# Batch 0's first 32 rows of a Fourier transform stored from even partitions, weights loaded behind these stores, and later casts of two constants

## The chip, the cores and the metric

The kernel runs on one core of one Trainium2 chip. The metric is device time in microseconds (us), lower is better. Work on the core is spread over TensorE (PE in the profile, its weight loads PEld), VectorE (DVE), ScalarE (ACT), GpSimd (POOL) and SyncE (SP), which here does nothing but issue DMAs. Each engine runs its own instructions in order; a DMA that SP has issued moves on 16 DMA engines while SP goes on to the next.

## What is computed

Eight batches of 3136 x 256 numbers go through a real Fourier transform along the 3136 rows, a complex 256 x 256 linear layer with bias and soft threshold, the inverse transform, and then a sparse feed-forward layer on the 128 rows with the highest score.

```python
X = np.fft.rfft(x, axis=1)
Yr = Xr @ w_r - Xi @ w_i + b_r;  Yi = Xr @ w_i + Xi @ w_r + b_i
Yr = np.sign(Yr) * np.maximum(np.abs(Yr) - lam, 0.0)      # Yi likewise
y = np.fft.irfft(Y, n=x.shape[1], axis=1)
# per batch: the 128 rows with the highest y @ w_gate
xe = y[b, top_idx];  h = np.maximum(xe @ w1, 0.0);  ye = h @ w2
out[b, top_idx] = xe + sigmoid(score)[:, None] * ye
```

## The kernel before, in words

**Stages.** 3136 is split as 49 x 64. For one batch, stage 1 (`s1`, matmuls of line 397) is a 49-point transform in 8 units `i` of [128 partitions x 8 x 128]; partitions 0 to 63 and 64 to 127 hold the two halves of the 256 columns, and in each half 49 rows are real and 15 are padding. Each unit is copied out of PSUM by ACT (line 412, half of it) and DVE (line 413, the other half) and stored to a scratch tensor `As` in DRAM, so that stage 2 can read it back with rows and columns exchanged (`av`, line 145). Stage 2 (`s2`, line 445, PSUM tile `px`) is the 64-point transform of a group `g` of four rows; there are 13 groups a batch, and one `av` pair (one DMA for each half) serves two groups. Its result is split into a rounded part `Xh` (ACT) and a rest `Xl` (DVE, and POOL for its negated copy), `spectral` multiplies it with the weights in three products each (lines 203 to 205, PSUM tile `py`), `shrink_a`, `shrink_b`, `shrink_c` add the bias, apply the threshold and split again into `Yh` and `Yl` (POOL), and `s2i` does the inverse 64-point transform with the table `gip` (PSUM tile `s`, again lines 203 to 205). `s1i` is the inverse 49-point transform. The feed-forward layer (`prepare`, `hidden`, `combine`) runs between these stages and at the end.

**Steps.** The main loop runs 104 steps `t`, one for each group of each batch. In step `t` PE does `s2` of group t + 1, `spectral` of group t and `s2i` of group t - 2, and from time to time units of `s1` for a later batch and of `s1i` for an earlier one. Inside the loop PE, ACT, DVE and SP are held to the order in which the code is written (`ordered`); POOL is not. `av` is loaded 3 steps ahead (`AP`), x units 4 steps (`XP`).

**The beginning.** Ahead of the loop SP issues, in this order: the 8 x units of batch 0, a piece of the stage-2 table `g_sb`, and then, as `s1` of batch 0 delivers its units, stores. Units 0 and 1 are stored whole (512 KB each). Of units 2 to 7 the rows 0 to 15 of each half are stored first, which is two DMAs of 16 partitions (64 KB) a unit, and the rows 16 to 63 later, two of 48 partitions (192 KB). The weights `w_r` (tile `r1`) and `w_i` (tile `Yl`) are loaded between the first stores. Then come x unit 1 of batch 1, the bias, and the first `av` pair, which reads rows 0 to 7 of all units and so has to wait for all of the first stores. `s1` of the units 0 and 1 of batch 1 and the split of the weights stand ahead of stage 2.

**The casts.** The inverse table `gip` is made in 7 pieces: a piece is loaded into a tile `gi` of one buffer, copied with rounding by ACT (line 174), and the rest is taken by POOL (line 175). At an odd step `t` the load, the ACT copy and the POOL instruction of a piece are written one after another. The same holds for the 8 pieces of `w2` (load into `xe`, ACT line 195, POOL line 196), one at every even step from 24 to 38.

Of the kernel before, what the change touches and what calls it, by code (L numbers as in the profile page):

```python
# [10 lines left out]
F32 = mybir.dt.float32  # L11
# [65 lines left out]


def _places():
# [17 lines left out]
def fourier_moe(ctx: ExitStack, tc: tile.TileContext, x, w_r, w_i, bri, wg, w1, w2,  # L97
# [69 lines left out]
    def ld_gi(k):  # L167
        s = slice(4 * k, min(4 * k + 4, NJ))
        t = pool.tile([128, s.stop - s.start, 128], F32, name="gi", bufs=1)
        ld(t, t_gi[:, s])  # L170
        return t, s

# [9 lines left out]
    def consts_moe(k):  # L182
# [6 lines left out]
        elif k == 1:  # L189
            ld(w1s, w1.rearrange("(h p) f -> p h f", p=128))  # L190
        else:
            f = k - 2
            t = pool.tile([128, D], F32, name="xe", bufs=3)
            ld(t, w2[128 * f:128 * f + 128])
            nc.scalar.copy(out=w2h[:, f, :], in_=t)
            nc.gpsimd.tensor_tensor(out=w2l[:, f, :], in0=t, in1=w2h[:, f, :].bitcast(F32), op=ALU.subtract)

# [206 lines left out]
    def s1(b, i):  # L404
        if i == 0:
            As[b] = dram.tile([2, 64, N2, 128], F32, name="As")
        n = ("at", "at", "at", "ct", "ct", "ot", "ot", "ot")[i] if b == 0 else "at"
        a = pool.tile([P, 8, 128], F32, name=n, bufs=2 if n == "ct" else 3)
        p = [ps.tile([P, 4, 128], F32, name="s", bufs=4) for _ in range(2)]
        xi = xt.pop((b, i))  # L410
        tiles4(p, w1f, lambda r, c: xi[64 * r:64 * r + N1, :, 128 * c:128 * c + 128])
        nc.scalar.copy(out=a[:, :4, :], in_=p[0])
        nc.vector.tensor_copy(a[:, 4:, :], p[1])  # L413
        if t >= 0:
            store(As[b].rearrange("h q n d -> (h q) n d")[:, 8 * i:8 * i + 8, :], a)
        else:
            made.append((b, i, a))

    made = []

    def st_a(b, i, a, q=slice(0, 64)):
        to = As[b][:, :, 8 * i:8 * i + 8, :]
        if q == slice(0, 64):
            ld(to.rearrange("h q n d -> (h q) n d"), a)
        else:
            for h in range(2):
                ld(to[h, q], a[64 * h + q.start:64 * h + q.stop])

    def ld_a(b, g):
        if g == G - 1:  # L430
            av[b, g] = pool.tile([64, 2, 1, 128], F32, name="av", bufs=3)
            ld(av[b, g][:, :, 0], As[b][:, N1 - 1].rearrange("h n d -> n h d"))
        elif g % 2 == 0:
            av[b, g] = av[b, g + 1] = pool.tile([128, 2, 4, 128], F32, name="av", bufs=3)
            for h in range(2):
                ld(av[b, g][:, h], As[b][h, 4 * g:4 * g + 8].rearrange("(j q) n d -> (q n) j d", q=2))

# [112 lines left out]
    HB, YB = 2, 3  # L550
    G, U, ORD = 13, 8, 0
    PE, ACT, DVE, SP = [getattr(mybir.EngineType, n) for n in ("PE", "Activation", "DVE", "SP")]
# [104 lines left out]
    loaded = [U + 2]  # L657
    ws = []

# [13 lines left out]
    t = -1  # L673
# [12 lines left out]
    s1(1, 0)  # L686
    s1(1, 1)
    split_w(ws[0], wrh, wrl)
    split_w(ws[1], wih, wil)
    add_bias()  # L690
    ld_a(0, 0)
    ld_a(0, 1)
    gi = ld_gi(0)
# [6 lines left out]
    for u in made[5:8]:  # L700
        st_a(*u, slice(16, 64))
    for u in made[8:]:
        st_a(*u)
    for t in range(-1, B * G):
# [123 lines left out]
```

## Time and profile before

| | |
|---|---|
| median of 3 runs | 713.37 us (712.81 to 713.53) |
| profiled execution, its own time | 713.84 us |
| its span | 712.1 us |
| PE busy | 676.7 us (95 %) |
| DVE, ACT, POOL busy | 468.1, 384.6, 210.0 us |
| mean granted clock of TensorE | 0.983 of 2.4 GHz |

The span is what the profile shows from the first instruction to the last; 1.74 us of the execution's own time lie around it. In the rows further down a `timeline` line gives start, duration, engine, line of the code, operation, output and inputs, and in brackets how long the engine stood idle just before and what ended that. A windows line gives for one stretch the busy time of PE, PEld, DVE, ACT and POOL (in brackets the count of instructions), then the granted clock of TensorE as a share of 2.4 GHz (0.50 is 1.2 GHz), the mean busy share of the 16 DMA engines, and GB/s moved. A chain line gives start, duration and what ran.

### The profile page before, as it was taken

The page shows a single profiled execution, that of the slowest core. Times are in us where ns is not written, and L with a number is a line of the kernel's source. Part 1 is how long each engine was busy: PE and PEld are TensorE (multiplying, and loading weights), DVE is VectorE, ACT ScalarE, POOL GpSimd, SP SyncE. Part 2 cuts the span into 40 slices and gives each one's busy share as a digit, 9 for nine tenths or more (in the row PEclk, how much of TensorE's full clock was granted, in tenths as well). Part 3 has the DMA queues.
Part 4 walks back from the last instruction along what each step waited for, and adds up shares of the span by engine and source line. Part 5 has one row for each costly group of instructions (what it writes and reads, how often), then busy time and mean ns, then how long its engine had stood idle before and what let it go on. Part 6 is the DMA issues. An engine that isn't in the chain of part 4 may idle for free.

```text
span 712.1 us, 15039 instructions
## 1 busy us (share of the span) xinstructions
PE 676.7 (95%) x5482; PEld 556.7 (78%) x5482; DVE 468.1 (66%) x1330; ACT 384.6 (54%) x759; POOL 210.0 (29%) x255
## 2 busy tenths in 40 slices
PE   7499999999999999999999999999999999998997
PEld 2288788998888689878987888887877887886666
DVE  3256666566655555565677877777897789966752
ACT  3145565565564665666666556665556454445541
POOL 1024433324332323322223322222322322232231
PEclk9689999999999899999999999999999999999999
DMA  9989987788789899989999999997877765646960
GB/s 334 303 299 343 357 247 232 245 276 274 243 301 331 287 318 314 328 292 343 327 299 298 333 321 316 305 307 244 260 239 223 221 206 185 196 158 219 379 238 24
DMA packets 146551, 195.29 MB, mean 274 GB/s; under 512 B 8725, under 2 KB 111278, under 8 KB 146478
## 3 DMA queue, kind: packets, MB, share of 16 engines
q1 hardware_dynamic: 145422, 192.10, 81.2%
q0 software_dynamic: 912, 2.21, 1.0%
q8 instruction: 43, 0.70, 0.4%
q14 instruction: 30, 0.25, 0.1%
q10 hardware_dynamic: 144, 0.03, 0.0%
HBM read 100.58 MB, written 93.85 MB: 273 GB/s over the span
## 4 chain that ended last, share of the span: by engine, by line
PE 72%; DVE 11%; DMA 7%; issue 4%; ACT 3%; POOL 1%; SPq 1%; POOLq 0%; DVEq 0%; ACTq 0%
PE s L397 13%; PE py L203 11%; PE py L204 11%; PE px L445 11%; PE py L205 11%; PE s L203 3%; PE s L204 3%; PE s L205 3%; DMA gi<-t_gi 3%; DVE py L472 2%; PE py L351 2%; DMA xe<-in_moe_w 2%; DVE yf L479 1%; DVE Xl L450 1%; PE s L351 1%
## 5 line engine op out<-in xcount | busy, mean ns | idle before, releaser
L487 POOL TENSOR_TENSOR Yl<-yf,Yh 128x512 fp32r<-128x512 f32 (+1 forms) x104 | 130.3, 1253 | 343.2 <-ACT Yh L486 337.0
L474 ACT ACTIVATE r<-py,m2l 128x512 f32<-128x512 f32 (+1 forms) x104 | 69.8, 671 | 157.4 <-DVE py L472 154.4
L472 DVE TENSOR_TENSOR py<-py,bias 128x512 f32<-128x512 f32 (+1 forms) x104 | 70.4, 676 | 106.0 <-PE py L205 100.9
L445 PEld LDWEIGHTS px<-g_sb,av 128*128 128x128 f32 (+1 forms) x800 | 99.7, 194 | 39.1 <-DVE at L413 20.8
L203 PE MATMUL py<-wrh,Xh 128*128 128x256 f32 x400 | 122.9, 307 | 0.0
L445 PE MATMUL px<-g_sb,av 128*128 128x128 f32 (+1 forms) x800 | 115.6, 287 | 5.9 <-DVE Xl L450 4.6
L204 PE MATMUL py<-wrh,Xl 128*128 128x256 f32 x400 | 113.3, 283 | 0.0
L205 PE MATMUL py<-wrl,Xh 128*128 128x256 f32 x400 | 113.2, 283 | 0.0
L203 PE MATMUL py<-wih,Xh 128*128 128x256 f32 x400 | 113.0, 282 | 0.0
L204 PE MATMUL py<-wih,Xl 128*128 128x256 f32 x400 | 112.9, 282 | 0.1
L205 PE MATMUL py<-wil,Xh 128*128 128x256 f32 x400 | 112.3, 281 | 0.0
L450 DVE TENSOR_TENSOR Xl<-px,Xh 128x512 fp32r<-128x512 f32 (+1 forms) x104 | 69.5, 669 | 42.9 <-ACT Xh L449 31.3
L518 DVE CUSTOM_DVE_ANT_0 junk<-ct,wgb 128x256 f32<-128x256 f32 (+1 forms) x200 | 90.6, 453 | 6.2 <-ACT ct L505 3.2
L505 ACT COPY ct<-s 128x512 f32<-128x512 f32 (+1 forms) x104 | 59.4, 572 | 52.3 <-PE s L205 50.4
L397 PE MATMUL s<-xt,w1f 49*64 49x512 f32 x480 | 68.5, 648 | 12.8 <-DMA xt<-in_x 7.8
L203 PEld LDWEIGHTS py<-wrh,Xh 128*128 128x128 f32 x400 | 76.5, 191 | 2.0 <-issue 1.0
L204 PEld LDWEIGHTS py<-wrh,Xl 128*128 128x128 f32 x400 | 76.6, 191 | 0.9 <-issue 0.9
L205 PEld LDWEIGHTS py<-wrl,Xh 128*128 128x128 f32 x400 | 76.4, 191 | 0.0
L204 PEld LDWEIGHTS py<-wih,Xl 128*128 128x128 f32 x400 | 76.0, 190 | 0.3 <-POOL Xl L451 0.3
L203 PEld LDWEIGHTS py<-wih,Xh 128*128 128x128 f32 x400 | 76.0, 190 | 0.0
L205 PEld LDWEIGHTS py<-wil,Xh 128*128 128x128 f32 x400 | 75.9, 190 | 0.0
L479 DVE SCALAR_TENSOR_TENSOR yf<-py,r 128x512 f32<-128x512 f32 (+1 forms) x104 | 69.5, 668 | 8.0 <-ACT r L474 4.2
(125 smaller groups left out, 1197.4 us busy)
## 6 DMA issues: line engine op xcount, KB each, us to landing
xt<-in_x SPq DMA_DIRECT2D x60, 512.0 KB, 6.1
As<-at SPq DMA_DIRECT2D x58, 512.0 KB, 4.1
cv<-As SPq DMA_DIRECT2D x58, 512.0 KB, 5.5
out<-ot SPq DMA_DIRECT2D x57, 512.0 KB, 3.6
av<-As SPq DMA_DIRECT2D x96, 256.0 KB, 5.0
As<-ct SPq DMA_DIRECT2D x96, 256.0 KB, 4.9
out<-at SPq DMA_DIRECT2D x7, 512.0 KB, 6.9
xt<-As SPq DMA_DIRECT2D x6, 512.0 KB, 5.3
```

The source lines that it names most:

```text
L203: nc.tensor.matmul(out, wh, mh, start=start, stop=False)
L204: nc.tensor.matmul(out, wl, mh, start=False, stop=False)
L205: return nc.tensor.matmul(out, wh, ml, start=False, stop=stop).ins
L397: last_mm = nc.tensor.matmul(out[r][64 * c:64 * c + 64], w[64 * r:64 * r + N1, :], src(r, c), start=True, stop=True)
L445: nc.tensor.matmul(px[:, 2 * p + h, :], a[:, h, 2 * (g % 2) * (w - 1) + p, :], g_sb[:r, 2 * g + p, :], start=True, stop=True)
L450: nc.vector.tensor_tensor(out=xl[:, :, NF:], in0=px, in1=xh[:, :, NF:].bitcast(F32), op=ALU.subtract)
L472: nc.vector.tensor_tensor(out=p, in0=p, in1=bias[:, :w, :], op=ALU.add)
L474: nc.scalar.activation(out=r1[b, g], in_=p, func=AF.Relu, bias=m2l, scale=1.0)
L479: nc.vector.scalar_tensor_tensor(out=yf, in0=py.pop((b, g)), scalar=0.0, in1=r1.pop((b, g)), op0=ALU.min, op1=ALU.add)
L487: nc.gpsimd.tensor_tensor(out=yl, in0=yf, in1=yh.bitcast(F32), op=ALU.subtract)
L505: nc.scalar.copy(out=c, in_=p)
L518: nc.vector.tensor_tensor_reduce(out=junk[:r], in0=c[:, k, :], in1=wgb[:r], scale=1.0, scalar=0.0, op0=ALU.mult, op1=ALU.add, accum_out=Cs ...
```

## The change

**Batch 0's stage 1** uses a second copy of its table, `w1p`, with the columns in another order (`_parity`): rows 0 to 31 of each half come out in the even partitions, rows 32 to 48 and the padding in the odd ones. `w1p` is loaded on ACT's queue ahead of `w1f`. The even partitions of a unit (64 partitions, 256 KB) are stored in one DMA to a DRAM tensor `early`, the odd ones later, in one DMA, to `late`. `av` of batch 0 reads from these. `As[0]` is left for the inverse; its padding rows are filled by two DRAM-to-DRAM copies (`pads`, 480 KB each) at steps 14 and 16.

**Order at the beginning.** All eight `early` stores come before the two weight loads, and the first `av` pair comes right behind the weights, ahead of x unit 1 of batch 1, the bias and the next piece of `g_sb`. `s1` of unit (1, 1) and the bias instructions move into step 0, behind `s2` of group 1.

**Casts.** A `gi` piece is loaded into one of the four buffers of `cv`; pieces 0 and 1 ahead of the loop, the others at steps 1, 3, 5, 7, 9. The ACT copy and POOL instruction of the next piece in line are written at the end of step 0 and of each odd step from 1 to 11, so from piece 2 on two steps behind the load. `w2` pieces are loaded as before and split at the end of steps 28, 30, ... 42, four steps behind the load. `gi` and `w2` casts are now in ACT's fixed order.

```diff
@@ s1, st_a, pads, ld_a
-        n = ("at", "at", "at", "ct", "ct", "ot", "ot", "ot")[i] if b == 0 else "at"
-        a = pool.tile([P, 8, 128], F32, name=n, bufs=2 if n == "ct" else 3)
+        n = ("at", "at", "at", "ct", "ct", "ot", "ot", "ot")[i] if b == 0 else "cv" if b == 1 and i < 2 else "at"
+        a = pool.tile([P, 8, 128], F32, name=n, bufs={"ct": 2, "cv": 4}.get(n, 3))
...
-        tiles4(p, w1f, lambda r, c: xi[64 * r:64 * r + N1, :, 128 * c:128 * c + 128])
+        tiles4(p, w1f if b else w1p, lambda r, c: xi[64 * r:64 * r + N1, :, 128 * c:128 * c + 128])
...
+    def st_a(i, k):
+        ld((early, late)[k].rearrange("h q n d -> (h q) n d")[:, 8 * i:8 * i + 8, :], made[i][k::2])
+
+    def pads(h):
+        ld(As[0][h, N1:].rearrange("p (i n) d -> i p (n d)", n=8), x[0, :, 64 * h + N1:64 * h + 64].rearrange("i p m d -> i p (m d)"))
...
+        src = As[b] if b else early if g < 8 else late
+        q = 4 * g - (0 if b or g < 8 else 32)
@@ ahead of the loop
         s1(0, i)
-        st_a(*made[-1], slice(0, 64 if i < 2 else 16))
-        if i < 2:
-            ws.append(ld_w(*((w_r, "r1", 1), (w_i, "Yl", YB))[i]))
-        if i == 0:
+        st_a(i, 0)
+        if i == 1:
             ld_x(1, 0)
+    ws = [ld_w(w_r, "r1", 1), ld_w(w_i, "Yl", YB)]
+    s1(1, 0)
+    split_w(ws[0], wrh, wrl)
+    split_w(ws[1], wih, wil)
+    ld_a(0, 0)
+    ld_a(0, 1)
     ld_x(1, 1)
     ld(bias, bri)
...
+    ld_gi(0)
+    for i in (3, 0, 1, 2, 4):
+        st_a(i, 1)
     ld(wgb, wg)
...
@@ the loop
-        if t % 2 and (t + 1) // 2 in range(1, 6):
-            consts_gi(*ld_gi((t + 1) // 2 + 1))
+        if t % 2 and (t + 3) // 2 in range(2, 7):
+            ld_gi((t + 3) // 2)
...
+        if t in (14, 16):
+            pads((t - 14) // 2)
...
-        if t < 0:
-            consts_gi(*gi)
-            consts_gi(*ld_gi(1))
+        if t == 0:
+            ordered(s1, 1, 1)
+            add_bias()
...
+        if t == 0 or t % 2 and (t + 1) // 2 in range(1, 7):
+            ordered(consts_gi, *gis.pop(0))
+        if t in range(28, 28 + 2 * (FF // 128), 2):
+            ordered(split_w2, (t - 28) // 2)
```

SP's order at the beginning, from the table piece to the first `av` pair, before (`r` and `Yl` are the weights, `As<-at`, `As<-ct` and `As<-ot` the stores):

```order
L145 DMA g_sb<-t_g 128x512
L145 DMA As<-at 128x1024
L145 DMA r_117<-in_w_r 128x2x256
L145 DMA xt<-in_x 128x1024
L145 DMA As<-at 128x1024
L145 DMA Yl<-in_w_i 128x2x256
L145 DMA As<-at 16x1024 x2
L145 DMA As<-ct 16x1024 x4
L145 DMA As<-ot 16x1024 x6
L145 DMA xt<-in_x 128x1024
L145 DMA bias<-in_b 128x512
L145 DMA av<-As 128x4x128 x2
```

And the same stretch now:

```order
L157 DMA g_sb<-t_g 128x512
L157 DMA early<-at 64x1024 x2
L157 DMA xt<-in_x 128x1024
L157 DMA early<-at 64x1024
L157 DMA early<-ct 64x1024 x2
L157 DMA early<-ot 64x1024 x3
L157 DMA r_193<-in_w_r 128x2x256
L157 DMA Yl<-in_w_i 128x2x256
L157 DMA av<-early 128x4x128 x2
L157 DMA xt<-in_x 128x1024
L157 DMA bias<-in_b 128x512
```

Fourteen stores became eight, the weights moved behind all of them, and x unit (1, 1) and the bias moved behind the `av` pair.

PE's order from batch 0's stage 1 to the first spectral product, before and then now (`s<-xt` and `s<-cv` are units of stage 1, four matmuls a unit; `px` is stage 2):

```order
L397 MATMUL s<-xt,w1f 64x512 x16
L397 MATMUL s<-cv,w1f 64x512 x16
L397 MATMUL s<-xt,w1f 64x512 x8
L445 MATMUL px<-g_sb,av 128x128 x8
L203 MATMUL py<-wrh,Xh 128x256
```

```order
L415 MATMUL s<-xt,w1p 64x512 x16
L415 MATMUL s<-cv,w1p 64x512 x16
L415 MATMUL s<-xt,w1f 64x512 x4
L463 MATMUL px<-g_sb,av 128x128 x8
L415 MATMUL s<-xt,w1f 64x512 x4
L221 MATMUL py<-wrh,Xh 128x256
```

Unit (1, 1) moved from ahead of the first two stage-2 groups to behind them; from there on PE's order is the same.

ACT's order around one `w2` cast of batch 2's part of the program (`at`: copy of a stage-1 unit, `ot`: copies of an inverse unit, `Xh`: split of `px`), before and then now:

```order
L474 ACTIVATE r_2762<-py,m2l 128x512
L412 COPY at<-s 128x512
L195 CAST w2h<-xe 128x256
L547 COPY ot<-s 128x4x128 x2
L448 CAST Xh<-px 128x4x128
```

```order
L492 ACTIVATE r_2754<-py,m2l 128x512
L430 COPY at<-s 128x512
L565 COPY ot<-s 128x4x128 x2
L466 CAST Xh<-px 128x4x128
L467 ACTIVATE Xh<-px 128x4x64
```

The cast that stood between the copies `at` and `ot` is gone from this place; the casts now stand at the ends of later steps.

## Rows read from the trace of the kernel before

**Rows 1.** The page, 40 slices of the span: clock granted to TensorE, in tenths.

```profile
PEclk9689999999999899999999999999999999999999
```

**Rows 2.** Windows by stage: PE, PEld, DVE, ACT, POOL busy; clock; DMA share; GB/s.

```profile
0.00:20.00 20.00, 14.04 (x72) 4.83 (x72) 6.93 (x17) 6.02 (x10) 1.82 (x10) 1.00 0.93 343
20.00:33.40 13.40, 4.36 (x16) 2.19 (x16) 3.47 (x6) 2.40 (x5) 1.26 (x1) 0.59 0.91 280
33.40:39.53 6.13, 6.12 (x28) 6.12 (x29) 0.69 (x1) 0.87 (x2) 0.81 (x2) 0.50 1.01 352
39.53:100.00 60.47, 56.94 (x470) 48.29 (x469) 37.76 (x77) 34.49 (x68) 24.09 (x26) 1.00 0.92 309
100.00:230.50 130.50, 130.22 (x1101) 115.58 (x1101) 80.11 (x195) 75.44 (x148) 45.21 (x56) 1.00 0.85 275
230.50:241.00 10.50, 9.81 (x43) 5.85 (x41) 3.88 (x9) 6.43 (x14) 3.90 (x5) 0.67 0.70 237
241.00:450.00 209.00, 208.63 (x1771) 174.57 (x1773) 141.39 (x358) 128.38 (x254) 60.83 (x75) 1.00 0.96 318
```

**Rows 3.** Timeline of SP's issues: stores and the first `av` pair.

```profile
10.42 0.33 SPq L145 DMA_DIRECT2D As<-at  x1
19.98 2.71 SPq L145 DMA_DIRECT2D As<-ot  x6
22.78 0.37 SPq L145 DMA_DIRECT2D xt<-in_x  x1
23.83 0.93 SPq L145 DMA_DIRECT2D av<-As  x2
```

**Rows 4.** Timeline of ACT and PE around the first stage-2 groups.

```profile
17.94 0.58 ACT L412 COPY ot<-s 128x512 f32<-128x512 f32 x1 [0.32 <-PE s L397]
29.97 1.65 PE L445 MATMUL px<-g_sb,av 128*128 128x128 f32 x6 [0.45 <-DMA av<-As]
33.41 2.08 PE L445 MATMUL px<-g_sb,av 128*128 128x128 f32 x8 [1.78 <-DVE Xl L450]
```

**Rows 5.** Windows at the beginning, same columns: the DMA queue around the first stores.

```profile
15.00:20.00 5.00, 3.98 (x30) 1.19 (x22) 3.20 (x6) 2.24 (x5) 0.00 (x0) 1.00 1.05 411
21.00:22.00 1.00, 0.00 (x0) 0.00 (x0) 0.69 (x1) 0.00 (x0) 0.00 (x0) 1.00 0.71 127
24.00:25.00 1.00, 0.00 (x0) 0.00 (x0) 0.00 (x0) 0.00 (x0) 0.00 (x0) 0.50 0.93 209
25.00:30.00 5.00, 2.73 (x11) 0.86 (x11) 1.12 (x2) 0.00 (x0) 0.00 (x0) 0.50 0.96 309
```

**Rows 6.** Timeline of ACT and PE where casts of `gip` wait for `gi`.

```profile
50.65 0.46 PE L445 MATMUL px<-g_sb,av 128*128 128x128 f32 x2 [0.46 <-DMA av<-As]
55.09 0.62 ACT L174 CAST gip<-gi 128x512 fp32r<-128x512 f32 x1 [2.20 <-DMA gi<-t_gi]
56.82 1.16 PE L445 MATMUL px<-g_sb,av 128*128 128x128 f32 x8 [1.05 <-DVE Xl L450]
87.06 1.16 PE L445 MATMUL px<-g_sb,av 128*128 128x128 f32 x8 [1.35 <-DVE Xl L450]
```

**Rows 7.** Timeline of PE and ACT around a `w2` cast.

```profile
230.95 2.09 PE L397 MATMUL s<-xt,w1f 49*64 49x512 f32 x8
231.02 0.40 ACT L195 CAST w2h<-xe 128x256 fp32r<-128x256 f32 x1 [4.42 <-DMA xe<-in_moe_w]
234.22 1.97 PE L397 MATMUL s<-cv,w1tf 49*64 49x512 f32 x4 [0.69 <-ACT ct L505]
241.00 0.28 PE L205 MATMUL s<-Yl,gip 128*128 128x256 f32 x1
```

**Rows 8.** From issue to landing, by tile: loads of `gi`, then of `xe`.

```profile
DMA to landing us min/median/max: 2.9/5.8/7.8
DMA to landing us min/median/max: 4.4/5.6/6.8
```

**Rows 9.** Chain: 16 undisturbed matmuls of line 397, two units.

```profile
256.20 1.88 PE s L397 x16
```

More of the change, by code (lines that the diff above doesn't have):

```diff
@@ L76, in _halves, with _parity @@
     return out.reshape(128, 64)
+def _parity(w):
+    out = np.zeros((N1, 64))
+    out[:, 0:64:2] = w[:, :32]
+    out[:, 1:2 * (N1 - 32):2] = w[:, 32:]
+    full = np.zeros((2, 64, 64))
+    full[:, :N1] = out
+    return full.reshape(128, 64)
 def _places():
@@ L114, in fourier_moe @@
     w1f, w1tf = c_tile([128, 64], F32, "w1f"), c_tile([128, 64], F32, "w1tf")
+    w1p = c_tile([128, 64], F32, "w1p")
+    nc.scalar.dma_start(out=w1p, in_=t_wf[2])
     nc.scalar.dma_start(out=w1f, in_=t_wf[0])
+    early, late = [dram.tile([2, 32, N2, 128], F32, name=n, bufs=1) for n in ("early", "late")]
     last = {}
@@ L168, in ld_gi @@
         s = slice(4 * k, min(4 * k + 4, NJ))
-        t = pool.tile([128, s.stop - s.start, 128], F32, name="gi", bufs=1)
+        t = pool.tile([P, 8, 128], F32, name="cv", bufs=4)[:, :s.stop - s.start, :]
         ld(t, t_gi[:, s])
-        return t, s
+        gis.append((t, s))
+    gis = []
     def consts_gi(t, s):
@@ L192, in consts_moe, with split_w2 @@
             f = k - 2
[L193 to L196, printed above, removed]
+            w2f.append(pool.tile([128, D], F32, name="xe", bufs=3))
+            ld(w2f[-1], w2[128 * f:128 * f + 128])
+    w2f = []
+    def split_w2(f):
+        nc.scalar.copy(out=w2h[:, f, :], in_=w2f[f])
+        nc.gpsimd.tensor_tensor(out=w2l[:, f, :], in0=w2f[f], in1=w2h[:, f, :].bitcast(F32), op=ALU.subtract)
     def pair(h_shape, tag, bufs):
@@ L382, in store @@
     def store(dst, src):
-        if t < 0:
+        if t < ORD:
             nc.sync.dma_start(out=dst, in_=src)
@@ L406, in s1 @@
             As[b] = dram.tile([2, 64, N2, 128], F32, name="As")
-        n = ("at", "at", "at", "ct", "ct", "ot", "ot", "ot")[i] if b == 0 else "at"
-        a = pool.tile([P, 8, 128], F32, name=n, bufs=2 if n == "ct" else 3)
+        n = ("at", "at", "at", "ct", "ct", "ot", "ot", "ot")[i] if b == 0 else "cv" if b == 1 and i < 2 else "at"
+        a = pool.tile([P, 8, 128], F32, name=n, bufs={"ct": 2, "cv": 4}.get(n, 3))
         p = [ps.tile([P, 4, 128], F32, name="s", bufs=4) for _ in range(2)]
         xi = xt.pop((b, i))
-        tiles4(p, w1f, lambda r, c: xi[64 * r:64 * r + N1, :, 128 * c:128 * c + 128])
+        tiles4(p, w1f if b else w1p, lambda r, c: xi[64 * r:64 * r + N1, :, 128 * c:128 * c + 128])
         nc.scalar.copy(out=a[:, :4, :], in_=p[0])
         nc.vector.tensor_copy(a[:, 4:, :], p[1])
-        if t >= 0:
+        if b > 0:
             store(As[b].rearrange("h q n d -> (h q) n d")[:, 8 * i:8 * i + 8, :], a)
         else:
-            made.append((b, i, a))
+            made.append(a)
     made = []
[L421 to L427, printed above, removed]
+    def st_a(i, k):
+        ld((early, late)[k].rearrange("h q n d -> (h q) n d")[:, 8 * i:8 * i + 8, :], made[i][k::2])
+    def pads(h):
+        ld(As[0][h, N1:].rearrange("p (i n) d -> i p (n d)", n=8), x[0, :, 64 * h + N1:64 * h + 64].rearrange("i p m d -> i p (m d)"))
     def ld_a(b, g):
+        src = As[b] if b else early if g < 8 else late
+        q = 4 * g - (0 if b or g < 8 else 32)
         if g == G - 1:
             av[b, g] = pool.tile([64, 2, 1, 128], F32, name="av", bufs=3)
-            ld(av[b, g][:, :, 0], As[b][:, N1 - 1].rearrange("h n d -> n h d"))
+            ld(av[b, g][:, :, 0], src[:, q].rearrange("h n d -> n h d"))
         elif g % 2 == 0:
@@ L550, in fourier_moe @@
     HB, YB = 2, 3
-    G, U, ORD = 13, 8, 0
+    G, U, ORD = 13, 8, -1
     PE, ACT, DVE, SP = [getattr(mybir.EngineType, n) for n in ("PE", "Activation", "DVE", "SP")]
@@ L657, in fourier_moe @@
     loaded = [U + 2]
-    ws = []
     def firsts(u):
@@ L678, in fourier_moe @@
         s1(0, i)
-        st_a(*made[-1], slice(0, 64 if i < 2 else 16))
-        if i < 2:
-            ws.append(ld_w(*((w_r, "r1", 1), (w_i, "Yl", YB))[i]))
-        if i == 0:
+        st_a(i, 0)
+        if i == 1:
             ld_x(1, 0)
+    ws = [ld_w(w_r, "r1", 1), ld_w(w_i, "Yl", YB)]
[4 more added lines that the diff above has]
+    ld_a(0, 1)
     ld_x(1, 1)
     ld(bias, bri)
[L686 to L693, printed above, removed]
     consts_g(1)
-    for u in made[2:5]:
-        st_a(*u, slice(16, 64))
     ld_a(0, 2)
     ld_a(0, 3)
+    ld_gi(0)
+    for i in (3, 0, 1, 2, 4):
+        st_a(i, 1)
     ld(wgb, wg)
[L700 to L703, printed above, removed]
+    ld_gi(1)
+    for i in (5, 6, 7):
+        st_a(i, 1)
     for t in range(-1, B * G):
```

5 lines of the change are left out of this document (2 added, 3 removed).

## Prediction

> **What bounds the kernel now.** I read the windows by stage first. From 100 us on PE is all but never idle: 0.28 us in 130, 0.37 us in 209 [rows 2]. There a microsecond comes only from PE's own time, and PE's instructions are the same before and after. What can be gained lies in three places that these rows single out: 20 to 39.5 us (PE busy 4.36 of 13.4 us, and up to 39.53 at a granted clock of 0.50, which is 1.2 GHz), 39.5 to 100 us (3.53 us idle), and 230.5 to 241 us (clock 0.67 on average). The page's clock row shows the same two dips and no other [rows 1]. Next I asked in each place what ended PE's idle time.
>
> At the beginning it is the first `av` pair. PE starts its last matmuls of stage-2 group 0 when the pair has landed, at 29.97 us [rows 4]. The pair is issued at 23.83 us, since SP is busy with six 16-partition stores until 22.69 us; these in turn start only at 19.98 us, when the queue has worked down to the store issued at 10.42 us [rows 3]. Yet the last unit of stage 1 was copied out by 17.94 + 0.58 = 18.52 us [rows 4]. From 20 us the queue is poorly used: 127 GB/s at a busy share of 0.71 with nothing but 16-partition stores under way, against 411 GB/s just before [rows 5].
>
> From 39.5 to 100 us two of PE's waits, 1.05 and 1.35 us, name DVE's `Xl`, but in front of the first ACT had waited 2.20 us for a `gi` load, with its copy for `Xl` queued behind the cast [rows 6]; in front of the second it is the same pattern. At 231 us ACT had waited 4.42 us for a `w2` load; PE first ran slowly, then stood 0.69 us, and from about there its clock is 0.50 for over 6 us [rows 2, 7].
>
> **The change, part by part.** *The beginning.* Stage 1 of batch 0 has the same instructions in the same order, so its last unit is still ready at 18.5 us and its `early` store is issued by 19 us. What must move before that store is done: 8 x units and one of batch 1 (9 x 0.52 MB), the table piece (0.26), eight early stores (8 x 0.26), some 0.2 of small tables: 7.3 MB. Before, 20 us x 343 GB/s = 6.9 MB had moved by 20.0 us [rows 2]; the remaining 0.4 MB at 411 GB/s [rows 5] takes 1 us, so the last byte moves at 21.0. A landing is seen later than that: the store issued at 10.42 us ends 6.6 MB, which the same count puts at 19.4 us, and SP saw it land at 19.98 [rows 3]; I add 0.6 and get 21.6 us. The weights (0.52 MB) are by then already in the queue and end at 22.3. The `av` pair is issued from 21.6 to 22.5 us (0.93 us for two [rows 3]). Bytes of a load begin about 1.2 us after its issue starts: the x unit issued at 22.78 is the first large load after the stores, and the queue is at 209 GB/s again in the window from 24 us [rows 3, 5]. From 22.8 us the pair's 0.52 MB takes 1.7 us (309 GB/s, the mean of 25 to 30 us, where the pair of before moved among others) to 2.5 us (209 GB/s) [rows 5], and 0.6 to 1.2 us pass to the landing: 25.1 to 26.5 us. I take 26.4, near the late end, because the early stores also have to be read back just after they were written and the queue is no emptier than before. That is 29.97 - 26.4 = 3.6 us earlier (bounds 2.5 to 4.8, the late one with a queue 1 us behind this count).
>
> The weights' split on DVE is four instructions; DVE's six of 20 to 33.4 us took 3.47 us [rows 2], so four take some 2.3 and end about 25 us, before group 0 leaves PSUM, so they cost nothing; without that cover they would cost what they are late. Behind group 0, group 1 waits 1.78 us for `Xl` as before [rows 4]. Then stands something new on PE's path: unit (1, 1) of stage 1, which before ran while PE waited for `av` anyway. It is half of 1.88 us [rows 9], 0.94 us at full clock. The clock: before, it is 0.50 until 39.53, 6.1 us after group 1 began [rows 2, 4]. I assume the same 6.1 us; PE then does as much work at the low clock as before, only another piece of it, and the 0.94 us is what is left. Net: 3.6 - 0.9 = **2.7 us earlier** at 39.5 us.
>
> By the Trainium skill ("DMA: Bandwidth & Descriptors", section Specifications) one core gets about 358 GB/s from HBM. This trace disagrees, with 411 GB/s held over 5 us [rows 5]; by the page's figure the 7.3 MB would take 20.3 us, the estimate for the landing would be near 23.5 us, and the forecast 1.9 us later.
>
> Does the queue keep up behind that? By the sizes of the DMAs in SP's order, 16.4 MB end with the pair that PE waits for at 50.65 us [rows 6]; now 15.9 MB do, since one store of batch 1 moved behind, which is 1.3 us at 0.39 MB a us. From 20 to 33.4 us the queue ran at 280 GB/s [rows 2], against the 343 of the stretch ahead of it a loss of 2.5 us, and the new order leaves most of this out. That puts this `av` pair at about 47.5 us, where PE needs it at 50.65 - 0.46 - 2.7 = 47.5. The wait of 0.46 us stays about as it is; its bounds are 0 and 1.5 us.
>
> *The later `gi` casts.* Four buffers instead of one, and two steps between load and cast. A step is some 6 us (104 steps in about 620 us), a `gi` load took at most 7.8 us to land [rows 8], so ACT no longer waits; the two PE waits, **2.4 us**, go. ACT and POOL execute the same casts, only later; ACT is busy 34.5 of 60.5 us there [rows 2], and the cast of 0.62 us [rows 6] at the end of a step has the next stage-2 matmuls as cover. Without that cover it would be 0.6 us in each of seven steps. The first cast now comes behind group 0's threshold, and `Yl` of group 0 waits for it on POOL (1.26 us, POOL's one instruction from 20 to 33.4 us [rows 2]), which PE needs only two steps later. Next late in this stretch would be the queue, with shares of 0.92 on average [rows 2]; by bytes, the `av` pairs beyond the one above are 8 us and more ahead of PE. Bounds: 1 to 3 us.
>
> *The later `w2` casts.* Loads land after 6.8 us at most [rows 8], and four steps are over 20 us. The stall at 231 us goes. Its price: between 230.95 and 241.00 us PE does 16 matmuls of line 397, normally 1.88 us [rows 7, 9], and then, from 234.22 + 1.97 = 236.19 us on, 4.81 us of work at half clock, 2.4 us at full clock. 10.05 - 1.88 - 2.40 = **5.7 us**. If the clock fell all the same, only the part before 236.19 would come back, 3.4 us less what the clock took of it (1 us): 2.4.
>
> *`pads`.* Two DRAM-to-DRAM copies, 0.98 MB in all, two issues of 0.4 us on SP. Behind each stand `ct` stores and an `av` pair that PE needs three steps later, and the queue is at a share of 0.85 there [rows 2]. At 275 GB/s they are 3.6 us of queue, against a lead of some 17 us. I take 0; bounds 0 and 1 us. `w1p` on ACT's queue delays `w1f`, which nobody needs before 18 us: 0. SP waits for it with one x issue, some 0.5 us, while 3 MB are queued: 0.
>
> Sum: 713.84 - 2.7 - 2.4 - 5.7 = 703.0 us against the profiled execution's own time. The median of the three runs is 0.47 us lower, so the forecast for the median is 702.6 us.
>
> **The rivals** (all against the median).
>
> *The clock falls once more.* From 230.95 us on PE did stage-1 and inverse stage-1 matmuls slowly, stood 0.69 us, and the clock went to 0.50, while idle times of 1.05 and 1.35 us at 56.8 and 87 us did not lower it [rows 2, 6, 7]. At about 47.5 us PE does two stage-1 units and then waits for `av`; if this wait grows past some 1 us, or if the stall at 231 us survives in part, 6.3 us at 1.2 GHz cost about 3.1 us: 705.7 us. Against it: the same place before, with 0.46 us, kept the clock. The Trainium skill ("TensorE: Matmul & The Clock Gate", section HAM oscillation) says that short bursts of matmuls between waits for DMA let the clock fall again and again; by it such a fall would come wherever bursts and waits alternate, and this trace shows that for one of the three places. Chance 0.17.
>
> *The beginning gives nothing.* The queue, not SP, is the limit up to 50 us: then PE waits at the next `av` pairs for what it gained, and the 0.94 us of unit (1, 1) is lost as well. 713.37 + 0.9 - 2.4 - 5.7 = 706.2 us. For it: a share of 1.01 from 33.4 to 39.5 us [rows 2]. Against it: the badly used queue at 21 to 25 us [rows 5]. Chance 0.13.
>
> *The casts don't do what they say.* ACT waits at the later place for the same loads, because the queue runs ahead of them with other things; only the beginning is gained: 710.7 us. Against it: landings of at most 7.8 and 6.8 us [rows 8]. Chance 0.06.
>
> *Slower: stores from every second partition.* No row shows one. If 64 partitions with gaps move at half the 411 GB/s, the 16 stores (4.2 MB) take 10.2 us of queue more, half of it before the first `av` pair and half before the pair that PE needs at 47.5 us. The first pair would land at 31.5, and the later one some 7 us behind the 50.65 of before, with 3 us more of low clock from the longer waits: +10 - 2.4 - 5.7 = +1.9, that is 715.3 us. It decides from a store of 256 KB taking over 1.2 us of the queue. For it: 16-partition stores moved 127 GB/s [rows 5]. Against it: these were paced by SP's issues, 0.45 us each, and whole-unit stores ran in the 411 GB/s. Chance 0.04.
>
> **How the numbers follow.** The forecast, 702.6 us, has 0.60; its own range is 700.3 to 704.8, from the bounds of its terms. The rivals above have 0.17, 0.13, 0.06 and 0.04. A range from 700.0 to 707.5 us takes in the forecast's case and the first two rivals and leaves out the other two and the rare ends, under 2 in 10. Some 0.2 % (1.4 us) is what a measurement of this kernel can tell from no change: all cases but the last lie below 711.9 us. Faster 0.93, same 0.03, slower 0.04.
>
> **What would show it.** The timeline of SP: the last `early` store issued at 19 us, the first `av` pair at 21 to 22.5. PE's first full stage-2 group ending near 28 us instead of 31.6, the clock back at 1.00 near 36 us. No wait of ACT for `gi` or `xe` above a few tenths. The page's clock row with one dip instead of two, and PE idle about 3.5 us less from 40 us to 241. I am wrong if the `av` pair lands after 28 us, if PE waits over 1.5 us for `av` near 47 us, or if a second dip of the clock shows anywhere.

## The result and the profile after

The changed kernel takes 702.12 us (median of 4 runs, 701.25 to 703.28), beside 713.45 us for the kernel before in the same comparison: a ratio of 0.9846 with a 95% interval from 0.9822 to 0.9869. The forecast was 702.6 us, so the total came out as forecast. Its parts did not, and most of what follows is about that. The profiled execution took 703.28 us, the longest of the four; its span is 701.5 us, 10.6 us under that of before.

The clock row of the page has one dip where [rows 1] have two, and in the windows by stage (columns as in [rows 2]) PE is idle 0.30 us from 39.53 to 100 us, where it was 3.53 us before:

```profile
PEclk9699999999999999999999999999999999999999
```

```profile
20.00:33.40 13.40, 4.88 (x25) 3.78 (x24) 4.10 (x7) 1.49 (x4) 0.40 (x1) 0.63 0.89 284
33.40:39.53 6.13, 6.13 (x37) 4.52 (x38) 1.72 (x3) 1.42 (x3) 0.40 (x1) 0.69 1.00 364
39.53:100.00 60.47, 60.17 (x505) 52.26 (x504) 37.38 (x86) 37.21 (x74) 26.38 (x29) 1.00 0.98 335
```

The timeline of SP answers to [rows 3]. The early stores are issued by 20 us and the first `av` pair at 23.15 us; the pair that PE needs for its fifth stage-2 group (group 4) is issued at 41.20 us:

```profile
17.67 2.21 SPq L157 DMA_DIRECT2D early<-ot  x3
19.94 0.58 SPq L157 DMA_DIRECT2D r<-in_w_r  x1
20.57 0.50 SPq L157 DMA_DIRECT2D Yl<-in_w_i  x1
23.15 0.92 SPq L157 DMA_DIRECT2D av<-early  x2
41.20 1.22 SPq L157 DMA_DIRECT2D av<-early  x2
```

The timeline of PE answers to [rows 4] and [rows 6] (start, length, and in brackets the idle time before it and what ended it):

```profile
27.27 2.30 PE L463 MATMUL px<-g_sb,av 128*128 128x128 f32 x8 [6.84 <-DMA av<-early]
31.26 2.07 PE L463 MATMUL px<-g_sb,av 128*128 128x128 f32 x8 [1.69 <-DVE Xl L468]
33.26 1.99 PE L415 MATMUL s<-xt,w1f 49*64 49x512 f32 x8
36.84 0.41 PE L222 MATMUL py<-wih,Xl 128*128 128x256 f32 x1
37.24 0.28 PE L221 MATMUL py<-wih,Xh 128*128 128x256 f32 x1
39.00 1.05 PE L463 MATMUL px<-g_sb,av 128*128 128x128 f32 x8
49.41 0.46 PE L463 MATMUL px<-g_sb,av 128*128 128x128 f32 x2
50.03 0.94 PE L463 MATMUL px<-g_sb,av 128*128 128x128 f32 x6 [0.17 <-DMA av<-early]
54.34 1.05 PE L463 MATMUL px<-g_sb,av 128*128 128x128 f32 x8
82.62 1.05 PE L463 MATMUL px<-g_sb,av 128*128 128x128 f32 x8
230.44 0.28 PE L223 MATMUL s<-Yl,gip 128*128 128x256 f32 x1
```

Since PE's order is nearly the same, the same matmuls can be laid side by side, and the difference of their starts is the lead that has been gained by then. Group 0 ends at 27.27 + 2.30 = 29.57 instead of 29.97 + 1.65 = 31.62 us [rows 4]: 2.05 us. Group 2 starts at 39.00; before, this row read:

```profile
40.01 1.05 PE L445 MATMUL px<-g_sb,av 128*128 128x128 f32 x8
```

That is a lead of 1.0 us. The two groups that waited for `Xl` in [rows 6] start at 54.34 instead of 56.82 (2.5 us) and at 82.62 instead of 87.06 (4.4 us); by 97 us the lead is 5.2. The matmul at 241.00 us of [rows 7] now starts at 230.44: 10.56 us, and at the end the lead is still 10.5. So between these two executions 1.0 to 1.3 us come from the beginning, 3.9 from the stretch of the `gi` casts and 5.4 from the `w2` stall. The sum of the prediction had 2.7, 2.4 and 5.7.

### The profile page after: what moved, and what is told of

It reads as the page before. It is cut to its first block, busy times and chain, and to the rows that moved or that the text cites. A ratio compares the mean times of both kernels' runs of the same rounds, so it can differ in the third digit from the quotient of the medians.

```text
span 701.5 us, 15027 instructions
## 1 busy us (share of the span) xinstructions
PE 670.2 (96%) x5482; PEld 552.9 (79%) x5482; DVE 464.8 (66%) x1330; ACT 384.3 (55%) x759; POOL 209.5 (30%) x255
## 4 chain that ended last, share of the span: by engine, by line
PE 79%; DVE 11%; issue 4%; DMA 3%; ACT 2%; POOL 0%; SPq 0%; POOLq 0%; DVEq 0%; ACTq 0%
PE s L415 16%; PE px L463 12%; PE py L221 12%; PE py L222 12%; PE py L223 12%; PE s L221 3%; PE s L222 3%; PE s L223 3%; DMA av<-early 2%; DVE py L490 2%; DVE junk L536 2%; DVE yf L497 1%; PE py L369 1%; DVE Xl L468 1%; PE s L369 1%
## 5 line engine op out<-in xcount | busy, mean ns | idle before, releaser
L536 DVE CUSTOM_DVE_ANT_0 junk<-ct,wgb 128x256 f32<-128x256 f32 (+1 forms) x200 | 86.5, 433 | 6.1 <-ACT ct L523 2.9
L466 ACT CAST Xh<-px 128x512 fp32r<-128x512 f32 (+1 forms) x104 | 59.6, 573 | 27.7 <-PE px L463 22.0
```

The source lines that it names most:

```text
L466: nc.scalar.copy(out=xh[:, :, NF:], in_=px)
L536: nc.vector.tensor_tensor_reduce(out=junk[:r], in0=c[:, k, :], in1=wgb[:r], scale=1.0, scalar=0.0, op0=ALU.mult, op1=ALU.add, accum_out=Cs ...
```

## Experiments

**Parts of the change alone.** Three kernels put the later casts into the kernel before, without the new beginning. The first has the `gi` casts:

```diff
-        t = pool.tile([128, s.stop - s.start, 128], F32, name="gi", bufs=1)
+        t = pool.tile([P, 8, 128], F32, name="cv", bufs=4)[:, :s.stop - s.start, :]
...
-            consts_gi(*ld_gi((t + 1) // 2 + 1))
+            ld_gi((t + 1) // 2 + 1)
...
+        if t == 0 or t % 2 and (t + 1) // 2 in range(1, 7):
+            ordered(consts_gi, *gis.pop(0))
```

> The kernel before with one part of the change alone: the gi pieces go into four buffers of cv and are cast at the end of a step, two steps after their load; nothing else. Lining up the same matmuls of the two traces, PE is 1.3 us ahead at the matmuls that start at 51.3 us before, and 5.1 us ahead from 97 us on. Theory (the casts give more than the two idle times, because PE also lost time in short gaps behind them): about 3.9 us, 709.5 us. Rival (the term of the prediction, only the idle times of 1.05 and 1.35 us): 2.4 us, 711.0 us. Rival (the gain between 50 and 100 us comes from the new order of the beginning, not from the casts): 713.4 us.

Measured: 710.5 us (before 713.3), a ratio of 0.9972 [0.9955, 0.9989]; 2.8 us. In the kernel before ACT waits for `gi` five times between 50 and 100 us; here it waits once, 1.83 us at 45.8 us. But PE now waits longer for the `av` pair of group 4:

```profile
51.46 0.46 PE L447 MATMUL px<-g_sb,av 128*128 128x128 f32 x2 [2.17 <-DMA av<-As]
52.28 0.94 PE L447 MATMUL px<-g_sb,av 128*128 128x128 f32 x6 [0.36 <-DMA av<-As]
```

In [rows 6] the wait at this place was 0.46 us (0.68 with a second one of 0.22 us for the other half of the pair); here the two make 2.53 us. The time alone cannot choose between the two first expectations; the trace says that a longer wait took part of the gain.

The second has the `w2` casts (at line 213 of the changed kernel they stand in a function of their own, called in step 28 + 2f instead of 24 + 2f):

```diff
-            nc.scalar.copy(out=w2h[:, f, :], in_=t)
-            nc.gpsimd.tensor_tensor(out=w2l[:, f, :], in0=t, in1=w2h[:, f, :].bitcast(F32), op=ALU.subtract)
...
+        if t in range(28, 28 + 2 * (FF // 128), 2):
+            ordered(split_w2, (t - 28) // 2)
```

> The kernel before with one part of the change alone: the w2 pieces are cast four steps after their load. Theory (the stall at 231 us goes with its dip of the clock): PE's lead between the two traces grows from 5.2 to 10.5 us there, so 5.4 us, 708.0 us, and no second dip in the clock row. Rival (the clock falls all the same): 2.4 us, 711.0 us, with the dip still there.

Measured: 708.5 us, 0.9955 [0.9925, 0.9986]; 4.8 us by the medians. Three of the five runs took 708.2 to 708.5 us, the other two 711.0 and 712.0, with a lower granted clock (0.979 and 0.981 on average, beside 0.984 to 0.986); the trace is of one of the three. From 225 to 245 us PE is busy all the time at full clock:

```profile
225.00:245.00 20.00, 20.00 (x171) 15.93 (x164) 11.82 (x31) 14.25 (x30) 6.60 (x9) 1.00 0.93 307
```

Lined up with the profile of before, the lead grows there from 0.0 to 5.4 us: in this execution the theory holds. But this execution also shows something on the way. Up to 100 us this kernel is the kernel before, instruction for instruction, and yet it was 1.8 us behind it from 61 to 85 us: PE waited longer at group 4, and its clock fell. At 97 us it was level again.

```profile
52.55 0.46 PE L449 MATMUL px<-g_sb,av 128*128 128x128 f32 x2 [1.51 <-DMA av<-As]
53.26 1.04 PE L449 MATMUL px<-g_sb,av 128*128 128x128 f32 x6 [0.25 <-DMA av<-As]
```

```profile
46.00:63.00 17.00, 15.24 (x115) 13.51 (x115) 9.11 (x19) 9.64 (x19) 6.54 (x7) 0.90 0.88 293
```

So at this place the same code waited 0.68 us in one execution and 1.76 us in another, and what is lost at group 4 comes out of the waits for `gi` behind it: had PE been on time, it would have waited there.

The third has both edits and nothing else.

> The kernel before with both kinds of later casts, and with the beginning as it was (same stores, same order of the loads). Theory (the beginning is worth only 1.3 us, what is read at 51.3 us): 3.9 + 5.4 = 9.3 us, 704.1 us, some 2 us above the changed kernel or less. Rival (the beginning is worth the 2.7 us of the prediction): 11.3 - 2.7 = 8.6 us, 704.8 us. Rival (the two casts' gains overlap, as a later stall eats part of the first): 706 us or more.

Measured: 708.0 us, 0.9921 [0.9895, 0.9947]; 5.3 us, so the parts do not add up (2.8 + 4.8 would be 7.6), and the third expectation holds. The whole change is 5.9 us better than this kernel. Lined up with the changed kernel, it is level (0.1 us) until 46 us and 5.2 us behind from 58 us on, and no more is lost later. All of it is one place: group 4 waits 2.75 us, and the clock falls. From 55 to 97 us, in turn, all three kernels with later `gi` casts gain the same on the kernel before, 3.93 us: the lead goes from -3.92 to 0.01 us here, from -0.96 to 2.97 with the `gi` casts alone, and from 1.27 to 5.20 in the changed kernel. So these casts are worth 3.9 us, as the first expectation of the first run had it, and what differs is where group 4 has left PE.

```profile
47.43 1.95 PE L403 MATMUL s<-xt,w1f 49*64 49x512 f32 x16
52.12 2.47 PE L451 MATMUL px<-g_sb,av 128*128 128x128 f32 x8 [2.75 <-DMA av<-As]
```

```profile
46.00:63.00 17.00, 14.20 (x97) 12.49 (x97) 7.33 (x18) 8.24 (x18) 5.77 (x6) 0.80 1.05 364
```

**The new beginning without the later `gi` casts.** The changed kernel with `gi` loaded into one buffer and cast behind its load, as before (the reverse of the first diff).

> The changed kernel with one part undone: the gi pieces are loaded into one buffer and cast right behind the load, as before. Measured so far: before 713.3, later gi casts alone 710.5, later w2 casts alone 708.5, both 708.0, all of the change 702.1 us. Theory (with the old gi casts the chain of gi loads sets the time at 97 us, and eats what PE has gained or lost until then: in the run with later w2 casts alone PE was 1.8 us late at 80 us and level with the kernel before at 97 us): the new beginning is worth nothing here, 708 to 709 us. Rival (the parts add up): 702.1 + 2.8 = 704.9 us.

Measured: 708.5 us (707.1 to 712.7), as much as with the `w2` casts alone: the theory holds, no gain of the beginning shows here. PE does not wait at group 4 and is even 1.3 us ahead of the changed kernel at 61 us. Then ACT waits for `gi`, PE for `Xl` behind it, and the clock falls once more (63 to 80 us: 0.90):

```profile
64.88 0.62 ACT L186 CAST gip<-gi 128x512 fp32r<-128x512 f32 x1 [5.28 <-DMA gi<-t_gi]
67.59 1.28 PE L461 MATMUL px<-g_sb,av 128*128 128x128 f32 x8 [3.50 <-DVE Xl L466]
```

With the `w2` casts in all four, then: neither 708.5, `gi` casts 708.0, beginning 708.5, both 702.1 us. The ratios, 0.9955, 0.9921, 0.9938 and 0.9846, say the same: the interval of the last lies below the other three, and those three overlap. In the traces either of the two alone gives its gain back at the other's place.

**What in the beginning does it.** The same order of loads and stores, but every `early` or `late` store of a unit as two DMAs of 32 neighbouring partitions:

```diff
-        ld((early, late)[k].rearrange("h q n d -> (h q) n d")[:, 8 * i:8 * i + 8, :], made[i][k::2])
+        for h in range(2):
+            ld((early, late)[k][h, :, 8 * i:8 * i + 8, :], made[i][64 * h + 32 * k:64 * h + 32 * k + 32])
```

> The changed kernel with another form of the stores of batch 0: stage 1 puts its rows out in their natural order, and every early or late store is two DMAs of 32 neighbouring partitions instead of one DMA of every second partition. The bytes, the order and the copies are the same. Theory (one DMA a unit is what lets SP be through with the early stores at 19.9 us): SP is 1 to 2 us later with them, the first av pair lands at 28.3 to 29.3 us instead of 27.3, px group 4 waits 1 us or more at 50 us, and the time is 703.5 to 707 us (the upper end if the clock falls at 50 us). Rival (only the order counts, not the form): 702.1 us, within 0.7.

Measured: 708.2 us, so all that the beginning had brought is lost, though the order of the loads and stores is the same. The sign is the theory's, the place is not: SP issues the first `av` pair at 21.61 us, earlier than in the changed kernel. What is late is the end of the `late` stores and all behind them, and in group 4 PE starts at 52.83 us instead of 49.41. To see whether neighbouring partitions are to blame, the next kernel also makes two DMAs, but of every second partition of each half, `made[i][64 * h + k:64 * h + 64:2]`.

> The changed kernel with every early or late store of a unit split into two DMAs, each of every second partition of one half (32 partitions, as many as in the run with neighbouring partitions, which took 708.2 us and whose queue fell to shares of 0.69 to 0.87 from 30 to 42 us). Theory (what costs there is the number of DMAs that SP has to issue, 32 instead of 16): 706 to 708.5 us and the same weak queue from 30 to 42 us. Rival (it is that a store reads from neighbouring partitions): 702.1 us within 0.8, a queue share of 0.95 or more there.

Measured: 709.7 us, 0.9959 [0.9939, 0.9979]. The rival is out: neighbouring partitions are not to blame, and two DMAs cost about the same in either form (the intervals of the two runs overlap). The queue is weak as in the theory, but the time lies 1.2 us above its range, and its cause, the number of DMAs, is only part of what the traces show. SP's timeline of the changed kernel (first three lines) and of this one (the others):

```profile
29.17 2.68 SPq L157 DMA_DIRECT2D late<-at  x3
34.25 2.12 SPq L157 DMA_DIRECT2D late<-ot  x3
37.82 2.82 SPq L157 DMA_DIRECT2D xt<-in_x  x3
```

```profile
31.02 4.70 SPq L157 DMA_DIRECT2D late<-at  x6
38.15 3.64 SPq L157 DMA_DIRECT2D late<-ot  x6
42.96 2.66 SPq L157 DMA_DIRECT2D xt<-in_x  x3
46.16 1.28 SPq L157 DMA_DIRECT2D av<-early  x2
```

Three stores of 256 KB take SP 2.68 and 2.12 us, pauses between them included, six of 128 KB 4.70 and 3.64 us. The x units start 5.1 us later, the pair of group 4 five. Meanwhile the queue runs low, from 36 to 39 us in the changed kernel and in this one:

```profile
36.00:39.00 3.00, 3.00 (x23) 3.00 (x23) 0.00 (x0) 0.00 (x0) 0.00 (x0) 0.80 0.98 358
```

```profile
36.00:39.00 3.00, 3.00 (x29) 3.00 (x26) 0.70 (x2) 0.59 (x1) 0.40 (x1) 1.00 0.78 188
```

The Trainium skill ("SBUF — State Buffer", section Door 1: The DMA port swizzle) says that a transfer's rate depends on how many of 16 ports its partitions reach; by its table a store of all even partitions reaches 16, and each half store in both of these kernels 8. The traces agree that half stores move more slowly. From 18 to 20 us in the changed kernel (first line) and from 20 to 23 us in this one (second line) all bytes move in pieces of 4 KB, there of an x unit and `early` stores, here of `early` stores:

```profile
18.00:20.00 2.00, 1.43 (x14) 0.24 (x8) 0.77 (x2) 1.09 (x2) 0.00 (x0) 1.00 0.96 387
20.00:23.00 3.00, 0.00 (x0) 0.00 (x0) 0.32 (x1) 0.27 (x1) 0.00 (x0) 0.50 0.89 202
```

The DMA engines are nearly as busy, and move half as much; by the trace's records a piece takes 159 ns there and 298 ns here (medians). So the number of DMAs is not the only reason. How much of the loss comes from it and how much from the slower bytes stays open: a kernel with 16 DMAs of 8 ports was not tried.

**The clock.** Seven matmuls on the g table, whose result is not used, fill PE's gap in the changed kernel:

```diff
+    warm = ps.tile([P, 4, 128], F32, name="m", bufs=1)
+    for _ in range(7):
+        nc.tensor.matmul(warm, g_sb[:, 0, :], g_sb[:, 0:4, :], start=True, stop=True)
```

> The changed kernel with seven matmuls on the g table added on PE while it waits for the first av pair (their result is not used), so that PE's clock has no reason to fall there. From 27.27 to about 36.8 us PE does some 7.9 us of work at a granted clock of 0.50, about 3.9 us of it lost. Theory (the DMA queue sets when px group 4 can start, at 50.0 us): PE is 3 to 4 us ahead until 46 us and then waits 3 us or more for x units or for av; the time is 701.7 us, within 0.6 of the changed kernel. Rival (PE sets it): the lead stays, 698.2 us.

Measured: 703.1 us (702.6 to 706.8), no gain. The clock still fell in this execution, for half as long. PE had a lead of 1.15 us on the changed kernel from 52 us, without a wait at group 4, whose pair was issued 1.4 us earlier here, at 39.79 us (why, the traces don't show). So the place has no fixed time of 50.0 us. Of the lead 0.44 us were kept: ACT and DVE waited until stores out of the `at` buffers had landed.

```profile
79.08 0.59 ACT L430 COPY at<-s 128x512 f32<-128x512 f32 x1 [1.93 <-DMA As<-at]
```

**One x unit ahead of the first `av` pair**, and unit (1, 1) computed in PE's gap:

```diff
+    ld_x(1, 1)
     s1(1, 0)
+    s1(1, 1)
...
-    ld_x(1, 1)
...
-            ordered(s1, 1, 1)
```

> The changed kernel with the x unit (1, 1) loaded ahead of the first av pair instead of behind it, and unit (1, 1) of stage 1 computed ahead of px group 0, in PE's gap. Theory (from 22 to 25 us the queue is at 178 to 194 GB/s, so that half a megabyte fits in there, and unit (1, 1) costs about 1.1 us on PE's path): the av pair lands at most 0.5 us later, px group 2 starts about 1 us earlier, px group 4 some 0.5 us earlier, 701.3 us (700.3 to 702.1). Rival (the x unit pushes the av pair back by its 1.3 us): 702.1 to 703.5 us.

Measured: 702.2 us, no difference, on the border of the two expectations. PE is 0.7 us ahead at 46 us, and group 4 takes it back, with waits of 0.66 and 0.32 us for its pair; so the reason is neither of the two: in this execution it is again the pair that sets group 4. With this, the matmuls in the gap, and the pair of groups 4 and 5 loaded right behind that of groups 2 and 3 (`ld_a(0, 4)`):

> As the run with unit (1, 1) ahead, and besides seven matmuls on the g table in PE's gap (their result is not used) and the av pair of groups 4 and 5 loaded right behind that of groups 2 and 3. Theory (these were the waits that came next: low clock up to 36.8 us, av at 50 us): the clock is low for 6.8 us or not at all, px group 4 does not wait, and a lead of 2 to 3 us holds to the end: 699 to 700 us. Rival (the queue has no room before 85 us; the stores of batch 1 free the at buffers late, and PE's lead shrinks at about 80 us as in the run with the matmuls alone, from 1.15 to 0.44 us): 701 to 702 us.

Measured: 705.4 us, worse than the changed kernel. The clock stays at 1.00 and PE is 4.9 us ahead at 46 us. Then it stands for an x unit and for a piece of the g table that the earlier pair has pushed back, the clock falls, and at 52 us it is 0.8 us behind:

```profile
45.51 1.64 PE L415 MATMUL s<-xt,w1f 49*64 49x512 f32 x8 [1.95 <-DMA xt<-in_x]
48.85 2.04 PE L465 MATMUL px<-g_sb,av 128*128 128x128 f32 x8 [1.69 <-DMA g_sb<-t_g]
```

**The loads in the order in which they are needed.** So what is needed first has to stand first in the queue. The kernel above with these moves:

```diff
-        for n in range(1 if u < 0 else U):
+        for n in range(1 if u < 1 else U):
...
-    for i in (5, 6, 7):
-        st_a(i, 1)
...
+        if t == 2:
+            for i in (5, 6, 7):
+                st_a(i, 1)
...
-        n = ... else "cv" if b == 1 and i < 2 else "at"
+        n = ... else "cv" if b == 1 and i < 2 else "ot" if b == 1 and i > 4 else "at"
```

> As the run with the matmuls in the gap and av of groups 4 and 5 loaded early (there PE was 4.9 us ahead at 46 us, then waited 1.95 us for an x unit and 1.69 us for a g piece, its clock fell at 46 us, and 0.8 us were lost in the end), with four moves in SP's order: only one x unit a step until px group 2, so that the g piece comes ahead of x units (1, 4) and (1, 5); the late stores of units 5 to 7 three steps later; and units (1, 5) to (1, 7) of stage 1 go into the ot buffers, which are free then. Theory (the queue's order, not its amount, made PE wait at 43 to 49 us): px group 4 starts at 45 to 47 us, the clock stays at 1.00, 699 us (698 to 700.5). Rival (the amount decides, the wait only moves to a place between 50 and 85 us): 701 to 704 us.

Measured: 699.8 us (698.2 to 701.2), 0.9826 [0.9781, 0.9871]. The time is the theory's, and so is the trace: group 4 starts at 44.20 us (forecast 45 to 47), no wait, and PE's lead on the changed kernel is 5.6 us from 55 to 115 us.

```profile
42.33 1.95 PE L415 MATMUL s<-xt,w1f 49*64 49x512 f32 x16
44.20 1.16 PE L465 MATMUL px<-g_sb,av 128*128 128x128 f32 x8
```

At 120 us 1.0 us of it is lost, and 1.6 us at 641 us, where the clock fell for 3.4 us in this execution; why there, I did not find. A fall of the same length at the same place of the program cost 1.6 us in two more executions, that of the `gi` casts alone (651 us) and that of the run before this one (647 us). The intervals of this kernel and of the changed one overlap, so that a gain over the changed kernel is not shown beyond the noise: it is 2.3 us by the medians, 1.4 us by the ratios, and the trace agrees with it. The same without the matmuls in the gap:

> As the run with SP's new order, without the matmuls in PE's gap: the clock is at 0.50 from about 23 to 37 us as in the changed kernel. Theory (PE then comes to px group 4 about 3 us later than with them, at 48 us, with no wait): 701 us, some 2 us above the run with the matmuls. Rival (the queue sets the time of both): both within 0.7 us of one another.

Measured: 701.0 us, 0.9840 [0.9797, 0.9883], with no wait at group 4 (47.98 us) and a lead of 1.85 us from 55 to 115 us, of which 1.0 us is lost at 120 us here too. The difference of the medians, 1.2 us, lies between the two expectations; in the two traces it is 3.8 us at 55 us, so PE and not the queue sets the time there, as in the theory. And the same as the version with the matmuls, but units 5 to 7 in the `at` buffers as before:

> As the run with SP's new order and the matmuls in PE's gap (699.8 us, PE 5.6 us ahead of the changed kernel at 52 to 115 us, 4.7 us from 130 us), but units (1, 5) to (1, 7) of stage 1 stay in the at buffers, as in the changed kernel. Theory (with PE this far ahead, ACT and DVE wait at about 75 us for stores out of the at buffers, and PE with them; the 1 us at 120 us has nothing to do with the ot buffers): the lead shrinks by 1 to 3 us between 65 and 85 us, 700.5 to 702 us. Rival (the stores land in time, the queue being in better order; what was lost at 120 us came from the use of ot): the lead holds, 698.5 to 699.5 us.

Measured: 702.6 us (700.2 to 703.4), 0.9842 [0.9820, 0.9863], somewhat above the theory's range. The theory's place and size hold, though PE is less far ahead in this execution than it assumed: the lead, 2.3 us in this execution since its clock fell at 27 us, goes to 0.8 us between 82 and 85 us, behind the wait below (from the list of ACT's waits: us in total, times, longest). On the loss at 120 us the rival is right: it shows in both traces with `ot` and is absent here.

```profile
ACT at L430 <- DMA As<-at: 2.7, 1, 2.7
```

## Why the prediction was right in sum, and where its steps failed

*The first `av` pair* is what I mis-sized first. The last early store is issued at 19.4 us, as forecast (19), but the pair only at 23.15 us, not at 21.6 to 22.5, and PE starts at 27.27, not at 26.4. The queue was no better used than before while SP waited for the landing: 284 against 280 GB/s from 20 to 33.4 us [rows 2]. And the reference was wrong: I counted from 29.97 us, the start of the last six matmuls of group 0 [rows 4], and passed over the two that had run before them on the first half of the pair, and over all eight now having to follow. By the ends of the group the gain is 2.05, not 3.6 us.

*Unit (1, 1)* takes 1.99 us on PE's path at half clock, and 1.15 us of the lead are gone behind it (2.15 at the start of group 1, 1.0 at group 2), where I had 0.94. *The clock* is back between 36.84 and 37.24 us, 5.6 to 6.0 us after group 1 began; 6.1 was assumed. Net 1.0 us at group 2 instead of 2.7.

*"Does the queue keep up"* failed. I put the pair of group 4 at 47.5 us, from the assumption that the new order leaves out most of a loss of 2.5 us in the queue; it landed at 50.03 us. That PE waited 0.17 us only is luck of a kind: PE was as late as the pair. The rival "the beginning gives nothing" was right that the queue sets this place: PE brought there 4.9 us earlier gained nothing until the queue's order was changed. With the matmuls alone, where the pair came earlier, PE did gain 1.15 us there, so it is not a fixed limit.

*The `gi` casts* were put at 2.4 us, the two idle times. They are worth 3.9: the lead grows by 1.6 us around the first (1.3 at 52 us, 2.9 at 61), by 1.6 around the second (4.5 at 88) and by 0.7 around a third (5.2 at 97), which I had passed over. Before it ACT had waited 1.82 us for the last piece of `gi`, as in front of the other two. The idle column also names the wait in front of one matmul and not the short gaps behind it. In the kernel before, two neighbours that start 0.36 us apart where others start 0.12 apart, and the third wait (last line):

```profile
58.53 0.28 PE L203 MATMUL py<-wih,Xh 128*128 128x256 f32 x1
58.89 0.39 PE L204 MATMUL py<-wih,Xl 128*128 128x256 f32 x1
92.12 1.05 PE L445 MATMUL px<-g_sb,av 128*128 128x128 f32 x7 [0.37 <-DVE Xl L450]
```

*The `w2` casts* were right: 5.7 forecast (the terms written there give 5.8), 5.4 in the lead, no dip. *`pads`*: the lead stays between 5.1 and 5.2 us from 97 to 220 us, so 0 was right.

*The sum* was right by luck, because errors cancel: in the two traces the beginning brings 1.4 us less than its term and the `gi` casts 1.5 us more. Run alone, the parts cancel in another way. The casts, 8.1 us by the sum, are worth 5.3 us without the new beginning, and the beginning, 2.7 us by the sum, is worth 5.9 us on top of them (713.3, 708.0, 702.1 us) and nothing without the `gi` casts. The step that failed is the adding up itself. I took the 0.46 us wait at group 4 in one execution (0.68 us with its second half) for what that code does there; it is 1.76 to 2.75 us in the three runs that share this beginning, with a dip of the clock in two. In the kernel before, this loss was hidden since PE had to wait for `gi` later anyway. With the `gi` casts moved it comes out, and what the new beginning does is to take it away: 16 DMAs store batch 0 where 26 did, and SP gets to the pair of group 4 earlier, at 41.20 us instead of 42.90 in the kernel before and 44.01 with both casts alone. The order alone does not do this: with the same order and 32 DMAs SP gets there at 44.82 us, and the time is 708.2 us. It takes the form of the stores; whether by their number or by their speed is open. "The clock falls once more" was thus the right rival for the casts alone, and wrong for the whole change. "Slower: stores from every second partition" was wrong: stage 1's stores moved among loads at 384 GB/s from 13 to 18 us. Its argument was wrong as well: the 16-partition stores of before were not only paced by SP, as a piece of 4 KB took 367 ns from 21 to 23 us (median) beside 159 ns in the stores of every second partition.

On the clock the Trainium skill ("TensorE: Matmul & The Clock Gate", section HAM oscillation) speaks of kernels whose clock falls in each wait for DMA behind a short burst. At group 4 the runs agree with it by and large: waits of 0.17 to 1.0 us behind the two stage-1 units left the clock at 1.00, waits of 1.8 to 3.3 us lowered it in four kernels, and one of 2.5 us (the `gi` casts alone) did not.

## What to carry to other kernels

Terms read from one trace add up only as long as no later wait takes over: before adding them, ask for each what the next wait behind it would absorb, and run the parts alone and together. A place where PE arrives just as its data lands is not free of cost because one execution shows a short wait; price it as a wait with its possible dip of the clock. Where one engine issues all loads and stores, look at their form as well as at their order: here one store of 64 even partitions instead of two of 32 partitions was worth 6.1 and 7.6 us with the order unchanged. And try the order by the time at which each is needed; here that gave 1 to 2 us more, within the noise.

## What the runs showed of the hardware that I had not expected

SP's time for a store does not follow its size: 0.33 us for one of 512 KB in the kernel before [rows 3], and, pauses included, 0.71 to 0.89 us for one of 256 KB and 0.61 to 0.78 us for one of 128 KB. A piece of 4 KB took 159 ns in stores of 64 even partitions and 298 ns in stores of 32 partitions of one half. The first 50 us of the kernel before gave waits of 0.68 and 1.76 us at the same matmuls in two executions, and 2.5 and 2.75 us in two more in which `gi` was loaded into other buffers. And a kernel whose clock stayed at 1.00 until 45.9 us, with PE 4.9 us ahead, was 3.3 us slower than the changed one, since PE then waited 1.95 and 1.69 us for loads that stood later in the queue; with the loads in another order it was 2.3 us faster by the medians.
